# Score products in three reduced-precision passes from the second unit on, and a smaller fixed cost for VectorE in the planner

## The chip, the core and the metric

The kernel runs on one core of a Trainium2 chip. The metric is the device time of one execution in microseconds (us). A core has a matrix engine (TensorE, PE in the profile, with its weight loads as PEld), VectorE (DVE), ScalarE (ACT), GpSimd (POOL) and a queue engine (SyncE, SP) that issues the transfers between main memory and the on-chip buffers. Every engine works through its own list of instructions in order and waits on semaphores where it needs the result of another.

## The reference

Causal attention for 4 batches and 12 heads over 448 positions with head size 64, and behind it a feed-forward layer with a hard-swish gate. All is float32.

```python
scores = scale * np.matmul(q, k.transpose(0, 1, 3, 2))
scores = np.where(mask, -1000000000.0, scores)
scores = scores - np.max(scores, axis=-1, keepdims=True)
attn = np.exp(scores)
attn = attn / (np.sum(attn, axis=-1, keepdims=True) + 1e-09)
attn_out = np.matmul(attn, v)
...
x = attn_out.transpose(0, 2, 1, 3).reshape(B * S, H * D)   # 1792 x 768
h = x @ w_in                                                # 768 x 2048
g = h * np.clip(h + 3.0, 0.0, 6.0) / 6.0
out = g @ w_out                                             # 2048 x 768
```

## The kernel before

**Groups and units.** The 1792 rows are cut into tiles of 112. Four groups of 448 rows (the columns of the matrix products) go through the feed-forward layer one after another; group 0 holds the first tile of each batch. Its attention (`first_pair`, six pairs of heads) makes the head of the program. The attention of the later groups is cut into units (`unit(g, p)`, six for each of groups 1 to 3, one for each pair of heads), and the program lays these between the matrix products of the groups before, so that TensorE has work all the time.

**A unit.** Loads of q and k into a buffer `qk` and of v into `vr`; score products in four blocks (two tiles of the unit at a time, two heads; lines 507 onwards) into PSUM banks (all PSUM tiles have the name `b`); a mask with a row minimum on VectorE (L555); exponentials on ScalarE (L562); row sums inverted on VectorE; probabilities scaled by them on GpSimd or VectorE (L582); transposed on TensorE (L594), copied out of PSUM, and multiplied by v on TensorE (L529). In a *raw* unit (`at < N_RAW`) the scores are plain float32 products of `qk`. In the other units ScalarE or GpSimd first rounds `qk` to a high half and VectorE or GpSimd subtracts that for a low half (both in the type fp32r), and the scores are three products: high by high, high by low, low by high.

**Feed-forward weights.** They come in *chunks*, 16 of `w_in` and 24 of `w_out` for each group; a chunk is counted here from 0 in group 0. In group 0 a chunk lands in two buffers `wd`, VectorE puts its bits in order in three steps of two instructions (L642, L644, L647, with a PSUM bank for what lies between), ScalarE casts it to `wh` (L284), GpSimd or VectorE subtracts for `wl` (L296), and TensorE multiplies (L668, L669, L670: three matmuls make a *triple*; a chunk of `w_in` takes six triples, 18 matmuls). After each chunk of `w_in` ScalarE makes a relu (L691) and VectorE the gate (L697), which gives the product's PSUM bank free; two products have a bank at a time.

**What sets the order.** Every operation has a due key, the engines that may take it (with a cost factor and a delay after which an engine may help), a planned duration, and the buffers that it needs. `Flow.run` plays the program through before it is built: an engine takes the due operation with the smallest key whose inputs and buffers are there. That gives each engine its list, which the chip then follows in order. Planned durations of VectorE come from `elem`, those of the mask have 0.2 us more. `unit` gets its keys from `T_EARLY` and the other constants. The plan is nothing but an order: what runs on the chip waits by semaphores, for the instructions themselves.

**Queues.** All loads and stores go out on SP in one order; SP's issue of a transfer waits until the transfer eight places before it has landed. Names: `d` is a common set of on-chip buffers, `gh` and `gl` hold the halves of the gated result (and, at first, q and k and v of group 0), `kept_w` is a copy of the ordered weights in main memory for the later groups, `r` a buffer for results taken out of PSUM, `prow` the row statistics.

Of the kernel before, what the change touches and what calls it, by code (L numbers as in the profile page):

```python
# [16 lines left out]
B, H, S, D = 4, 12, 448, 64  # L17
DM, DFF = 768, 2048
C = 112
# [8 lines left out]

T_FIRST, T_EARLY, T_EACH, T_LATE, T_DENSE, T_LOAD, T_W, T_WLOAD = -66, 8, 13, 84, 7, -24, 9, 9
T_XA, T_X, T_LAST, T_PAIR, T_SUMS = 156, 178, 192, 10.5, 190
T_SECOND, T_PRODUCT = T_LAST + 8 * T_PAIR, 12

N_RAW = 7
T_V, T_W0 = 9,23
NORM_LAG = 1

BUFS = dict(
    gh=1, gl=1, prow=4, r=4, kl=3, vr=3, wh=3, wl=3, pr2=3, pr1=3, wd=6, d=22,  # L40
# [5 lines left out]
    qk="d qk", op="d op", wf="d wf", x="d x", pt="d pt", pr3="d pr3", xq="d xq", xc="d xc", gt="d gt", so="d so",  # L46
    ps="b s most ps", tp="b s most", av="b s", mo="b mo", c="b c",
)
MOST = dict(qk=4, op=4, wf=4, x=8, pt=5, pr3=2, xq=6, xc=21, gt=12, so=3, s=6, most=6, ps=6, mo=2, c=8)

ORDERED = dict(wd=0, wh=1, wl=2, xq=3, xc=3, gt=3, pr3=4, pr2=5, pr1=6, pt=7, op=8)

# [176 lines left out]
def tile_causal_attention_hardswish_moe(ctx: ExitStack, tc: tile.TileContext, q, k, v, w_in, w_out, out):  # L229
    nc = tc.nc  # L230
# [14 lines left out]

    flow = Flow({**BUFS, **BANKS, **MOST})

    def buf(tag, shape, dt=F32):
        return Buf(tag, shape, dt)

    def bank(tag):
        return Buf(tag, [128, 512], F32)

    def ap(b):
        if b.tile is None:
            b.tile = pools[b.tag].tile(b.shape, b.dt, tag=b.tag, name=b.tag)
        return b.tile
# [5 lines left out]
    def one(key, ways, dur, emit, r, w, port=True):  # L263

        ways = {e: x if isinstance(x, tuple) else (x, 0) for e, x in ways.items()}
        o = flow.op(key, ways, [(dur, emit, w)], r)
        if not port:
            o.port = set()

    def pe(key, parts, r, tiled=False):  # L270
        flow.op(key, {"PE": (1, 0)}, [(d, lambda e, g=g: g(), w) for d, g, w in parts], r, tiled)
# [3 lines left out]
        flow.op(key, {queue: (1, 0)}, [(0.1, lambda e: start(out=o(), in_=i()), w)], r, nbytes=nbytes)  # L275

    def elem(n, psum=False):
        return (n + 150) / 960

    def move(key, n, o, i, r, w, ways=None, scale=None):  # L280

        def emit(e):
            if e == "A":
                nc.scalar.copy(o(), i()) if scale is None else nc.scalar.mul(o(), i(), scale)  # L284
            elif e == "D":
                if scale is None:
                    nc.vector.tensor_copy(o(), i())
                else:
                    nc.vector.tensor_scalar(o(), i(), scale, None, ALU.mult)
            else:  # L290
                nc.gpsimd.tensor_scalar(o(), i(), 1.0, 1.0, ALU.mult, ALU.mult)
        one(key, ways or {"A": 1}, (n + 200) / 1200, emit, r, w)

    def minus(key, n, o, a, b, r, w, ways, op=ALU.subtract):
        def emit(e):
            (nc.gpsimd if e == "P" else nc.vector).tensor_tensor(o(), a(), b(), op)  # L296
        one(key, ways, elem(n), emit, r, w)
# [43 lines left out]
    def first_pair(p):  # L341
# [36 lines left out]
        for e in (1, 0):  # L378
            one(
                t + 1, {"D": 1}, elem(S), lambda _, e=e: nc.vector.tensor_reduce(row(e, 0), sc[e](), AX.X, ALU.max),  # L380
                [(ps[e], 0)], [(st, e, 0)],
            )
            if e:
                one(
                    t + 1, {"D": 1}, .25,
                    lambda _: nc.vector.tensor_scalar(row(1, 0), row(1, 0), -0.125, None, ALU.mult),
                    [], [(st, 1, 0)], False,
                )
        for b in range(B):
# [8 lines left out]
        allb = [(pr, 0, b) for b in range(B)]  # L398
        one(
            t + 2, {"D": 1}, elem(S), lambda _: nc.vector.tensor_tensor(pb[0](), sc[0](), wide(0, 0), ALU.subtract),  # L400
            [(ps[0], 0), (st, 0, 0)], allb,
        )
# [56 lines left out]
    def row_of(pr, e, i):  # L459
        x = ap(pr[e, i])  # L460
        return x[:, e] if i == NC_ - 1 else x

    def unit(g, p):
        at = NPAIR * (g - 1) + p
        raw32 = at < N_RAW
        t = T_EARLY + T_EACH * at if g == 1 else T_LATE + T_DENSE * (at - NPAIR)
        av, off = bank("av"), 0
        stages, turns, pieces, deps = [], [], [], []
        for u, (b, tiles, groups) in enumerate(UNITS[g]):
# [3 lines left out]
            qk = buf("qk", [128, R + S])  # L473
            for src, c0, c1, n in ((q, C * lo, 0, nq), (k, 0, nq, nk)):
                for h in range(2):
# [3 lines left out]
                        w=[(qk, h, bool(c1))],  # L479
# [4 lines left out]
            if not raw32:  # L484
                hi_lo, key = [buf("op", [128, R + S], F32R) for _ in range(2)], t - 5 + 2 * u
# [6 lines left out]
            st = buf("prow", [C, 2, 8])  # L492
            ps = {(e, i): bank("ps") for i in tiles for e in range(2)}
# [19 lines left out]
            pt = {}  # L513
            pairs = [buf("pt", [C, 2, S]) for _ in groups]
            for e in range(2):
                for js, ph in zip(groups, pairs):
                    blocks = [(i, j) for j in js for i in range(max(j, lo), hi)]
                    o = 0
                    for j in js:
                        w = C * (hi - max(j, lo))  # L520
# [18 lines left out]
        for a in range(0, len(stages), 2):  # L539
            two, key = stages[a:a + 2], t + a  # L540
            cost, more = (1.68e-3, .17) if raw32 else (1.362e-3, .05)
            for few in [two]:
                pe(
                    key,
                    [(cost * C * (i + 1) + more, lambda i=i, go=go: go(i), [(ps[0, i], 0), (ps[1, i], 0), ("turn",)])
                     for _, i, go, ps, *_ in few],
                    [x for z in few for x in z[6]] + [("unit", at - 2)], True,
                )
            for u, i, _, ps, pr, st, *_ in two:
                w = C * (i + 1)  # L550
                for e in range(2):
                    dst = lambda e=e, i=i, w=w, ps=ps: ap(ps[e, i])[:C, :w]
                    one(
                        key + .1, {"D": 1}, elem(w) + .2,
                        lambda _, e=e, i=i, w=w, dst=dst, st=st: nc.vector.tensor_tensor_reduce(  # L555
                            dst(), dst(), mask[:, S - w:], -0.125, 3.0e38, ALU.add, ALU.min, ap(st)[:, e, i:i + 1]
                        ),
                        [], [(ps[e, i], 0), (st, e, i)],
                    )
                    one(  # L560
                        key + .2, {"A": 1}, (w + 300) / 1200 + .25,
                        lambda _, e=e, i=i, dst=dst, st=st, pr=pr: nc.scalar.activation(  # L562
                            row_of(pr, e, i), dst(), ACTF.Exp, bias=ap(st)[:, e, i:i + 1], scale=-1.0,
                            accum_out=ap(st)[:, e, 4 + i:5 + i],
                        ),
                        [(ps[e, i], 0), (st, e, i)], [(pr[e, i], e), (st, e, 4 + i)],
                    )

        for u, (b, tiles, _) in enumerate(UNITS[g]):
            st, pr = [(z[5], z[4]) for z in stages if z[0] == u][0]  # L570

            def inverse(_, st=st, tiles=tiles):
                r = ap(st)[:, :, 4 + tiles[-1]:5 + tiles[0]]
                nc.vector.tensor_scalar_add(r, r, 1e-9)
                nc.vector.reciprocal(r, r)  # L575

            one(t + 4, {"D": 1}, .45, inverse, [], [(st, e, 4 + i) for e in range(2) for i in tiles], False)
            for e in range(2):
                for i in reversed(tiles):
                    def scaled(w, e=e, i=i, st=st, pr=pr):  # L580
                        x = row_of(pr, e, i)
                        (nc.gpsimd if w == "P" else nc.vector).tensor_scalar(  # L582
                            x, x, ap(st)[:, e, 4 + i:5 + i], 1.0, ALU.mult, ALU.mult
                        )
                    one(
                        t + 4.5 + .1 * e + .2 * u, {"P": 1, "D": (.6, NORM_LAG)}, .2 + C * (i + 1) / 1000, scaled,
                        [(st, e, 4 + i)], [(pr[e, i], e)],
                    )
        for c, (e, u, blocks, pr, ph, w, st) in enumerate(turns):
            tp, key = bank("tp"), t + 6 + .9 * c  # L590

            def turn(e=e, blocks=blocks, tp=tp, pr=pr):
                for o, (i, j) in enumerate(blocks):
                    nc.tensor.transpose(ap(tp)[:C, C * o:C * o + C], row_of(pr, e, i)[:, C * j:C * j + C], ident)  # L594

            pe(key, [(.1 * len(blocks), turn, [(tp, 0)])], [(pr[e, i], e) for i in sorted({i for i, _ in blocks})])
            move(
                key + .1, w, lambda ph=ph, e=e, w=w: ap(ph)[:, e, :w], lambda tp=tp, w=w: ap(tp)[:C, :w],
                [(tp, 0)], [(ph, e)], {"A": 1} if raw32 else {"A": 1, "D": (1, .4)},
            )  # L600
        pe(t + 15.9, pieces, deps, True)
        if g < 2:
# [436 lines left out]
    for g in range(2):  # L1039
        if g:  # L1040
            for p in range(NPAIR):
                unit(g, p)
        group(g)
    for g in (2, 3):
        for p in range(NPAIR):
            unit(g, p)
# [7 lines left out]
    with tc.manual_schedule():  # L1054
        for _, _, e, emit, port in order:
            traced = nc.cur_bb.bb.instructions
            n = len(traced)
# [42 lines left out]
```

## Time and profile before

| what | value |
|---|---|
| median of 3 runs | 613.27 us (612.43 to 614.84) |
| the profiled execution's own time | 614.25 us |
| its span in the trace | 612.5 us |
| mean granted TensorE clock | 0.989 |
| TensorE busy | 599.6 us, 98% of the span |
| VectorE busy | 470.2 us, 77% |
| ScalarE busy | 365.9 us, 60% |
| GpSimd busy | 269.1 us, 44% |

The span is what the trace covers; the run's own time has 1.75 us more around it. [...]

### The profile page before, as it was taken

To read this page: it belongs to the slowest core of one execution; us is meant where nothing else is said; L and a number is where in the kernel's file an instruction comes from. 1 tells how busy PE (TensorE), PEld (TensorE's weight loads), DVE (VectorE), ACT (ScalarE), POOL (GpSimd) and SP (SyncE) were. 2 spreads that over 40 slices of the span, in tenths; PEclk is the share of its full clock that TensorE was granted. 3 is DMA by queue.
4 is the path that set the end of the run, shared out by engine and by line. 5 is a ranking of instruction groups with operands and counts; after the bars stand their busy time and mean duration, and the time that the engine had idled before them with its cause. 6 is when DMAs were issued, how large, how long until landed. Compare 5 with 4: busy or idle time off the path is not lost.

```text
span 612.5 us, 11307 instructions
## 1 busy us (share of the span) xinstructions
PE 599.6 (98%) x3724; PEld 522.2 (85%) x3724; DVE 470.2 (77%) x1044; ACT 365.9 (60%) x846; POOL 269.1 (44%) x277
## 2 busy tenths in 40 slices
PE   7799999999999999999999999999999999999997
PEld 5577888887888888888888888899999999999996
DVE  5879987887796876688786755588778878898861
ACT  3955757655555767776576655375545575446630
POOL 1767785654676347655184161005554343010000
PEclk8979999999999999999999999999999999999999
DMA  9969986988898654444365344435554367583321
GB/s 207 258 176 331 336 270 229 331 254 287 262 289 255 196 172 143 138 137 142 109 173 166 118 127 133 126 117 176 166 167 162 121 196 241 164 261 114 116 68 54
DMA packets 79738, 114.68 MB, mean 187 GB/s; under 512 B 20736, under 2 KB 55488, under 8 KB 79680
## 3 DMA queue, kind: packets, MB, share of 16 engines
q1 hardware_dynamic: 79248, 113.80, 61.2%
q8 instruction: 29, 0.48, 0.3%
q14 instruction: 29, 0.24, 0.1%
q10 hardware_dynamic: 432, 0.17, 0.1%
HBM read 86.80 MB, written 27.13 MB: 186 GB/s over the span
## 4 chain that ended last, share of the span: by engine, by line
PE 92%; DMA 2%; DVE 2%; ACT 2%; POOL 1%; SPq 1%; issue 0%; DVEq 0%; POOLq 0%
PE b L668 24%; PE b L669 23%; PE b L670 23%; PE b L594 7%; PE b L507 7%; PE b L529 7%; DMA gh<-in_k_dram 1%; SPq L275 1%; DMA wd<-in_w_in_dram 1%; PE b L430 1%; ACT d L284 0%; PE b L373 0%; ACT d L392 0%; POOL d L582 0%; POOL d L421 0%
## 5 line engine op out<-in xcount | busy, mean ns | idle before, releaser
L668 PE MATMUL b<-d,wh 128*128 128x448 f32 x504 | 187.4, 372 | 1.0 <-DVE r L697 1.0
L669 PE MATMUL b<-d,wh 128*128 128x448 f32 x504 | 182.9, 363 | 0.0
L670 PE MATMUL b<-d,wl 128*128 128x448 f32 x504 | 182.2, 361 | 0.0
L284 ACT CAST wh<-wd 128x768 fp32r<-128x768 f32 (+1 forms) x92 | 71.5, 778 | 59.1 <-PE b L669 35.2
L668 PEld LDWEIGHTS b<-d,wh 128*128 128x128 f32 x504 | 94.7, 188 | 10.0 <-DVE r L697 1.4
L670 PEld LDWEIGHTS b<-d,wl 128*128 128x128 f32 x504 | 94.4, 187 | 7.0 <-POOL wl L296 0.3
L669 PEld LDWEIGHTS b<-d,wh 128*128 128x128 f32 x504 | 94.8, 188 | 5.0
L555 DVE CUSTOM_DVE_ANT_0 b<-b,mask 112x448 f32<-112x448 f32 (+2 forms) x144 | 69.5, 533 | 29.8 <-PE b L507 29.1
L296 DVE TENSOR_TENSOR wl<-wd,wh 128x768 fp32r<-128x768 f32 (+1 forms) x67 | 59.9, 894 | 32.3 <-ACT wh L284 31.4
L668 PE MATMUL b<-gh,wh 128*128 128x448 f32 x192 | 74.6, 388 | 0.0
L296 POOL TENSOR_TENSOR wl<-d,wh 128x512 fp32r<-128x512 f32 (+1 forms) x38 | 58.5, 1540 | 30.0 <-ACT wh L284 28.7
L670 PE MATMUL b<-gh,wl 128*128 128x448 f32 x192 | 69.7, 363 | 0.0
L669 PE MATMUL b<-gl,wh 128*128 128x448 f32 x192 | 69.7, 363 | 0.0
L296 POOL TENSOR_TENSOR wl<-wd,wh 128x768 fp32r<-128x768 f32 (+1 forms) x25 | 43.5, 1741 | 59.1 <-DVE vr L948 43.5
L284 ACT COPY d<-b 112x336 f32<-112x336 f32 (+2 forms) x110 | 46.5, 454 | 35.5 <-PE b L594 22.1
L562 ACT ACTIVATE pr<-b,prow 112x336 f32<-112x336 f32 (+1 forms) x96 | 47.0, 497 | 9.6 <-DVE prow L555 6.3
L507 PE MATMUL b<-d 64*112 64x448 f32 (+2 forms) x376 | 46.7, 376 | 0.4 <-DVE prow L414 0.4
L582 POOL TENSOR_SCALAR pr<-pr,prow 112x224 f32<-112x224 f32 (+1 forms) x69 | 33.9, 503 | 29.3 <-DVE prow L575 19.7
L529 PE MATMUL b<-d,vr 112*64 112x224 f32 (+2 forms) x504 | 44.9, 329 | 0.0
L529 PEld LDWEIGHTS b<-d,vr 112*64 112x64 f32 x504 | 30.6, 137 | 15.6 <-issue 2.6
L296 POOL TENSOR_TENSOR d<-d 128x560 fp32r<-128x560 f32 (+3 forms) x19 | 28.0, 1473 | 35.9 <-PE b L507 18.3
L594 PE MATMUL b<-ident,pr 112*112 112x112 f32 x240 | 43.2, 262 | 0.0
(110 smaller groups left out, 1072.4 us busy)
## 6 DMA issues: line engine op xcount, KB each, us to landing
wd<-in_w_in_dram SPq DMA_DIRECT2D x32, 384.0 KB, 5.9
wd<-in_w_out_dram SPq DMA_DIRECT2D x24, 512.0 KB, 5.4
wd<-kept_w SPq DMA_DIRECT2D x32, 384.0 KB, 3.5
wd<-kept_w SPq DMA_DIRECT2D x84, 128.0 KB, 3.1
kept_w<-d SPq DMA_DIRECT2D x16, 384.0 KB, 6.5
kept_w<-d SPq DMA_DIRECT2D x24, 256.0 KB, 5.4
wd<-kept_w SPq DMA_DIRECT2D x24, 256.0 KB, 2.8
kept_s<-wd SPq DMA_DIRECT2D x12, 512.0 KB, 3.5
```

What stands on the lines that cost most here:

```text
L275: flow.op(key, {queue: (1, 0)}, [(0.1, lambda e: start(out=o(), in_=i()), w)], r, nbytes=nbytes)
L284: nc.scalar.copy(o(), i()) if scale is None else nc.scalar.mul(o(), i(), scale)
L296: (nc.gpsimd if e == "P" else nc.vector).tensor_tensor(o(), a(), b(), op)
L507: nc.tensor.matmul(ap(ps[e, i])[:C, :w], x[m, c], y[m, nq:nq + w], start=n == 0, stop=n == len(terms) - 1)
L529: nc.tensor.matmul(ap(av)[64 * e:64 * e + 64, off + nq - w:off + nq], ap(vr)[:, j, e, :], ap(ph)[:, e, o:o + w], start=(j == 0), stop=(j = ...
L555: lambda _, e=e, i=i, w=w, dst=dst, st=st: nc.vector.tensor_tensor_reduce(dst(), dst(), mask[:, S - w:], -0.125, 3.0e38, ALU.add, ALU.min, ...
L562: lambda _, e=e, i=i, dst=dst, st=st, pr=pr: nc.scalar.activation(row_of(pr, e, i), dst(), ACTF.Exp, bias=ap(st)[:, e, i:i + 1], scale=-1. ...
L582: (nc.gpsimd if w == "P" else nc.vector).tensor_scalar(x, x, ap(st)[:, e, 4 + i:5 + i], 1.0, ALU.mult, ALU.mult)
L594: nc.tensor.transpose(ap(tp)[:C, C * o:C * o + C], row_of(pr, e, i)[:, C * j:C * j + C], ident)
L668: nc.tensor.matmul(ps, ap(wh)[:, a], xh, start=start, stop=False, skip_group_check=more)
L669: nc.tensor.matmul(ps, ap(wh)[:, a], xl, start=False, stop=False, skip_group_check=more)
L670: nc.tensor.matmul(ps, ap(wl)[:, a], xh, start=False, stop=stop, skip_group_check=more)
```

## The change

The scores of units 1 to 6 become three products of halves, as units 7 to 17 have them already; unit 0 alone stays raw. The planner's fixed part for a VectorE instruction goes from 150 to 130 elements (at 960 elements a microsecond) and the extra of a mask from 0.2 to 0.12 us. Some due keys move by 1 to 4, VectorE may help with scalings after 1.5 instead of 1, and with the copies of a raw unit's transposed tiles too; a ScalarE way for scalings is there with a delay of 99, which it never reaches; one more buffer pair `pt` may be held.

```diff
-T_FIRST, T_EARLY, T_EACH, T_LATE, T_DENSE, T_LOAD, T_W, T_WLOAD = -66, 8, 13, 84, 7, -24, 9, 9
-T_XA, T_X, T_LAST, T_PAIR, T_SUMS = 156, 178, 192, 10.5, 190
+T_FIRST, T_EARLY, T_EACH, T_LATE, T_DENSE, T_LOAD, T_W, T_WLOAD = -66, 5, 13, 80, 7, -24, 9, 8
+T_XA, T_X, T_LAST, T_PAIR, T_SUMS = 154, 177, 192, 10.5, 188
...
-N_RAW = 7
+N_RAW = 1
...
-NORM_LAG = 1
+NORM_LAG, NORM_LAG_A, TP_LAG, TP_LAG_RAW = 1.5, 99, 0.4, 0.4
+
+FIXED, ROWS = 130, 0.12
...
-MOST = dict(qk=4, op=4, wf=4, x=8, pt=5, pr3=2, xq=6, xc=21, gt=12, so=3, s=6, most=6, ps=6, mo=2, c=8)
+MOST = dict(qk=4, op=4, wf=4, x=8, pt=6, pr3=2, xq=6, xc=21, gt=12, so=3, s=6, most=6, ps=6, mo=2, c=8)
...
     def elem(n, psum=False):
-        return (n + 150) / 960
+        return (n + FIXED) / 960
...
-                        key + .1, {"D": 1}, elem(w) + .2,
+                        key + .1, {"D": 1}, elem(w) + ROWS,
...
-                        t + 4.5 + .1 * e + .2 * u, {"P": 1, "D": (.6, NORM_LAG)}, .2 + C * (i + 1) / 1000, scaled,
+                        t + 4.5 + .1 * e + .2 * u, {"P": 1, "D": (.6, NORM_LAG), "A": (1, NORM_LAG_A)}, .2 + C * (i + 1) / 1000, scaled,
...
-                [(tp, 0)], [(ph, e)], {"A": 1} if raw32 else {"A": 1, "D": (1, .4)},
+                [(tp, 0)], [(ph, e)], {"A": 1, "D": (1, TP_LAG_RAW if raw32 else TP_LAG)},
```

The lists of the engines move all over the program, since the plan is played anew. Line numbers in the changed kernel are 2 higher up to the masks (L509 for the score products) and 5 higher behind them (L647, L649, L652 for the bit steps, L673 to L675 for the weight products, L702 for the gate).

On VectorE, at the end of the head, where chunks 3 and 4 are put in order; before:

```order
L642 TENSOR_SCALAR b<-wd 128x384 x2
L644 SCALAR_TENSOR_TENSOR b<-wd,b 128x384 x2
L647 SCALAR_TENSOR_TENSOR d<-wd,b 128x384 x2
L697 SCALAR_TENSOR_TENSOR r<-r,b 128x448
L642 TENSOR_SCALAR b<-wd 128x384 x2
L644 SCALAR_TENSOR_TENSOR b<-wd,b 128x384 x2
L647 SCALAR_TENSOR_TENSOR d<-wd,b 128x384 x2
L697 SCALAR_TENSOR_TENSOR r<-r,b 128x448
L555 ISA b,prow<-b,mask 112x224
```

The same place on VectorE in the changed kernel, first the steps of chunk 3, then those of chunk 4:

```order
L289 CAST d<-b 128x448
L647 TENSOR_SCALAR b<-wd 128x384 x2
L649 SCALAR_TENSOR_TENSOR b<-wd,b 128x384 x2
L652 SCALAR_TENSOR_TENSOR d<-wd,b 128x384 x2
L647 TENSOR_SCALAR b<-wd 128x384 x2
L649 SCALAR_TENSOR_TENSOR b<-wd,b 128x384 x2
L652 SCALAR_TENSOR_TENSOR d<-wd,b 128x384 x2
L702 SCALAR_TENSOR_TENSOR r<-r,b 128x448 x2
L557 ISA b,prow<-b,mask 112x224
```

The gates of chunks 0 and 1 stood behind chunk 3 and behind chunk 4; now both stand behind chunk 4, and a cast of attention results stands ahead.

On TensorE, at the four last score products of unit 0 and the first triple of chunk 2 behind them; before (in brackets the engines and transfer queues whose semaphores the instruction waits for):

```order
L507 MATMUL b<-d 112x224 [waits Activation_49]
L507 MATMUL b<-d 112x224 [waits DVE_49]
L507 MATMUL b<-d 112x224 [waits DMAHW7_49,DMAHW5_49,Activation_49]
L507 MATMUL b<-d 112x224 [waits DMAHW6_49,DMAHW0_49,Activation_49]
L668 MATMUL b<-d,wh 128x448 [waits DVE_49]
L669 MATMUL b<-d,wh 128x448
L670 MATMUL b<-d,wl 128x448 [waits Pool_49]
```

The same place on TensorE in the changed kernel:

```order
L509 MATMUL b<-d 112x224 [waits Activation_49] x2
L509 MATMUL b<-d 112x224 [waits DMAHW7_49,DMAHW5_49,DVE_49]
L509 MATMUL b<-d 112x224 [waits DMAHW0_49,DMAHW6_49,DVE_49,PE_49]
L673 MATMUL b<-d,wh 128x448 [waits DVE_49,PE_49]
L674 MATMUL b<-d,wh 128x448
L675 MATMUL b<-d,wl 128x448
```

The counts behind these semaphores say for which instruction: before, L668 waits for the first gate (L697); now the third and the fourth score product wait for the two last bit steps of chunk 3 (L652), and L673 for the first L652 of chunk 4, whose PSUM bank it takes over. Ahead of this place TensorE has the same 36 matmuls of chunks 0 and 1; before, 12 triples stood behind all work of the head, and now 2 triples each stand ahead of and behind the first score products of unit 0, and 8 behind the head.

On TensorE, one of the blocks of scores of unit 1 (tiles of 448 and 336 columns), before and then in the changed kernel, from the two lists:

```order
L507 MATMUL b<-d 112x448 [waits DMAHW4_49,DMAHW2_49,Activation_49]
L507 MATMUL b<-d 112x448 [waits DMAHW5_49,DMAHW3_49,Activation_49]
L507 MATMUL b<-d 112x336 [waits DVE_49] x2
```

```order
L509 MATMUL b<-d 112x448 x6
L509 MATMUL b<-d 112x336 [waits Activation_49] x2
L509 MATMUL b<-d 112x336 x4
```

Four float32 products became twelve products of halves, and the transfers that the first waited for are now waited for by the engine that makes the halves.

## Rows read from the trace of the kernel before

**Rows 1.** The page, its first part: busy time, share of the span, instructions.

```profile
PE 599.6 (98%) x3724; PEld 522.2 (85%) x3724; DVE 470.2 (77%) x1044; ACT 365.9 (60%) x846; POOL 269.1 (44%) x277
```

**Rows 2.** Busy time by stage: stretch, its length, each engine, granted clock, DMA share, GB/s.

```profile
0.00:38.56 38.56, 30.58 (x260) 23.03 (x260) 29.04 (x70) 22.87 (x77) 18.28 (x24) 0.82 0.90 209
38.56:47.98 9.42, 8.43 (x47) 7.31 (x45) 5.97 (x13) 6.11 (x16) 5.63 (x4) 1.00 0.84 274
47.98:388.91 340.93, 340.72 (x2322) 286.12 (x2322) 264.05 (x680) 219.59 (x558) 189.11 (x203) 1.00 0.66 207
```

**Rows 3.** Timeline of TensorE: start, duration, instruction, [idle before and its releaser].

```profile
45.97 1.01 PE L507 MATMUL b<-d 64*112 64x224 f32 x8
47.98 0.48 PE L668 MATMUL b<-d,wh 128*128 128x448 f32 x1 [0.99 <-DVE r L697]
```

**Rows 4.** Timeline of TensorE around two blocks of float32 scores.

```profile
55.38 1.57 PE L507 MATMUL b<-d 64*112 64x448 f32 x8
56.89 0.47 PE L668 MATMUL b<-d,wh 128*128 128x448 f32 x1
57.20 0.36 PE L669 MATMUL b<-d,wh 128*128 128x448 f32 x1
...
73.75 1.01 PE L507 MATMUL b<-d 64*112 64x224 f32 x8
74.70 0.50 PE L529 MATMUL b<-d,vr 112*64 112x336 f32 x2
```

**Rows 5.** Timeline of TensorE around two blocks of three-product scores.

```profile
244.78 1.31 PE L507 MATMUL b<-d 64*112 64x448 f32 x12
246.02 0.31 PE L594 MATMUL b<-ident,pr 112*112 112x112 f32 x1
...
246.39 0.45 PE L668 MATMUL b<-d,wh 128*128 128x448 f32 x1
246.68 0.37 PE L669 MATMUL b<-d,wh 128*128 128x448 f32 x1
...
268.73 1.02 PE L507 MATMUL b<-d 64*112 64x336 f32 x12
269.68 0.50 PE L594 MATMUL b<-ident,pr 112*112 112x112 f32 x3
```

**Rows 6.** Timeline of VectorE where chunk 3 is put in order.

```profile
43.35 0.56 DVE L642 TENSOR_SCALAR b<-wd 128x384 int32<-128x384 int32 x1 [1.90 <-DMA wd<-in_w_in_dram]
44.98 0.56 DVE L642 TENSOR_SCALAR b<-wd 128x384 int32<-128x384 int32 x1 [1.06 <-DMA wd<-in_w_in_dram]
45.45 1.02 DVE L644 SCALAR_TENSOR_TENSOR b<-wd,b 128x384 int32<-128x384 int32 x2
46.38 1.01 DVE L647 SCALAR_TENSOR_TENSOR d<-wd,b 128x384 int32<-128x384 int32 x2
47.31 0.61 DVE L697 SCALAR_TENSOR_TENSOR r<-r,b 128x448 f32<-128x448 f32 x1
```

**Rows 7.** Timeline of the SP queue: the two issues of chunk 4.

```profile
41.12 1.16 SPq L275 DMA_DIRECT2D wd<-in_w_in_dram  x2
```

**Rows 8.** The page, part 6: issues, size of one, median us to landing.

```profile
wd<-in_w_in_dram SPq DMA_DIRECT2D x32, 384.0 KB, 5.9
```

**Rows 9.** Timeline of GpSimd: the low halves of the last attention results of group 0.

```profile
40.04 2.28 POOL L296 TENSOR_TENSOR d<-r,d 128x448 fp32r<-128x448 f32 x2
```

**Rows 10.** Busy time in windows of 4 us around the head's end, columns as in Rows 2.

```profile
28.00:32.00 4.00, 2.14 (x21) 1.38 (x17) 2.73 (x8) 3.45 (x11) 2.98 (x4) 0.78 0.58 142
32.00:36.00 4.00, 4.00 (x13) 2.71 (x14) 4.00 (x10) 0.00 (x0) 3.56 (x3) 0.50 0.44 105
36.00:40.00 4.00, 4.00 (x44) 3.48 (x43) 2.76 (x10) 3.65 (x8) 1.78 (x1) 0.87 0.51 144
...
44.00:48.00 4.00, 3.01 (x20) 2.23 (x18) 3.02 (x7) 1.79 (x3) 0.85 (x1) 1.00 1.02 404
```

**Rows 11.** Busy time in the first 12 us after the head, columns as in Rows 2.

```profile
49.00:61.00 12.00, 12.00 (x62) 10.20 (x60) 11.97 (x31) 6.91 (x18) 10.62 (x10) 1.00 0.87 310
```

More of the change, by code (lines that the diff above doesn't have):

```diff
@@ L581, in scaled @@
                         x = row_of(pr, e, i)
+                        if w == "A":
+                            nc.scalar.mul(x, x, ap(st)[:, e, 4 + i:5 + i])
+                            return
                         (nc.gpsimd if w == "P" else nc.vector).tensor_scalar(
```

## The prediction

> **What bounds the kernel now.** I read the page's busy times first. TensorE is busy for 98% of the span, VectorE for 77%, the others less [rows 1]. That is an average, so I cut the span into stages next, by the place where TensorE last waits. In the head, to 38.56 us, TensorE is busy for 30.58 us; in the next 9.42 us for 8.43; and from 47.98 to 388.91 us for 340.72 of 340.93 [rows 2]. So from 48 us on, everything on TensorE's list is paid for in full, an instruction saved there is time saved, and work of other engines costs nothing as long as it doesn't make TensorE wait. Ahead of 48 us it is the other way round: TensorE waits for others, and its list is short of work. The last of these waits is the one to look at. At 45.97 TensorE begins the four last score products of unit 0, and at 47.98 chunk 2 begins, 0.99 us late, released by VectorE's gate [rows 3]. Whatever moves the start of chunk 2 moves all that comes after it.
>
> **The scores on TensorE.** A block of float32 scores with tiles of 448 and 336 columns goes from 55.38 to the next instruction at 56.89, 1.51 us; one with 224 and 224 from 73.75 to 74.70, 0.95 us [rows 4]. Three products take 1.24 us for 448 and 336 columns (244.78 to 246.02) and 0.95 us for 336 and 224 (268.73 to 269.68) [rows 5]. For 224 and 224 no row exists. From 784 to 560 columns the time falls by 0.29 us, 1.3 ns a column, so 448 columns should take 0.95 - 112 x 0.0013 = 0.80 us. A unit of the first group of units then saves 0.27 + 0.15 = 0.42 us. Unit 6 has blocks of another cut, and I give it the same. Six units save 2.5 us. The bound below is what the first block alone saves, 6 x 0.27 = 1.6 us; the bound above has the small block save as much as the big one, 6 x 0.54 = 3.2 us.
>
> The order of TensorE's work changes too: the weight matmuls stand in 105 runs instead of 107, and the transpositions in 77 instead of 89. The first matmul of a run takes longer to the next one's start: 0.31 us behind scores (56.89 to 57.20) and 0.29 us behind transpositions (246.39 to 246.68) [rows 4, 5], so it hardly matters which work stands ahead. I put that at plus 0.1 us, and the whole at **-2.4 us**.
>
> [...]
>
> **VectorE ahead of chunk 2.** This is the place that I think decides. In the trace the two halves of chunk 3 land just ahead of 43.35 and 44.98, since VectorE's first steps on them begin there after waits for the transfer, and the six steps run until the gate of chunk 0 begins at 47.31 [rows 6]. In the changed list that gate stands behind the six steps of chunk 4 as well. Nor does chunk 4 come sooner: its two loads are issued from 41.12 on [rows 7], the order of the SP queue is the same up to there, and a load of these takes 5.9 us to land [rows 8], so the halves come at about 47.0 and 47.6, when VectorE is just through with chunk 3. Steps follow each other at 0.93 us for two, 0.465 us each (45.45, 46.38, 47.31 [rows 6]).
>
> What chunk 2's first matmul needs is, by the semaphore's count, the first L652 of chunk 4, whose PSUM bank it takes. That is the fifth step: it begins at 47.31 + 4 x 0.465 = 49.17 and ends 0.56 us later, at 49.73 (the 0.56 us is the duration of a single step [rows 6]). With a semaphore's passing chunk 2 begins at 49.8 instead of 47.98: **+1.8 us**. At most it waits for the gate of chunk 0 (47.31 + 6 x 0.465 + 0.61 = 50.7: +2.7 us); at least the banks are had in time, which is a rival below.
>
> Is TensorE there in time? Ahead of this place it has the same 36 matmuls and the same score products. The low halves of the last attention results are written by GpSimd until 42.3 (40.04 + 2.28 [rows 9]); behind them stand at most 12 triple parts of the two chunks, 12 matmuls at 0.2 us (57.20, and so on at the pace of [rows 4]), so TensorE could be through with the 36 by about 44.7. In the trace they end at 45.97, when the scores begin [rows 3]. So TensorE is not late, it is up to 1.3 us early, and waits the longer. The four score products don't shorten that: by their counts the third and the fourth wait for the last steps of chunk 3, which begin at 46.38.
>
> **The clock.** From 44.7 to 49.8 TensorE then has only the 0.95 us of scores, some 4 us of waiting. In the head the granted clock fell from 1.00 to 0.78, 0.50 and 0.87 in three windows of 4 us. This came in and behind a window in which TensorE was busy for 2.14 of 4 us; in the window 44 to 48, with 3.01 us busy, it stayed at 1.00 [rows 10]. The changed kernel's windows there come to about 1.7 us busy, nearer to the first. The fall in the trace is worth (0.22 + 0.50 + 0.13) x 4 = 3.4 us of full-speed work, if TensorE has work all through it; part of it lies in the waits that caused it. I take **+3.0 us**, with bounds 0 (the clock stays) and 3.4.
>
> **The other engines.** Units 1 to 6 need 12 casts on ScalarE and GpSimd and 12 subtractions (9 on GpSimd, 3 on VectorE), of which no row prices the effect on TensorE. They're hidden as long as the ordered weights are ready before TensorE wants them. That cover is thin right behind the head: from 49 to 61 us VectorE is busy for 11.97 of 12 us and GpSimd for 10.62 [rows 11]. By the two lists VectorE gets ten more items there before the steps of chunk 9: two casts, a copy, a subtraction and six scalings. But TensorE comes there 2 to 5 us late itself, which gives them as much. I take 0; without that cover they cost what they last, at most 10 x 0.6 = 6 us with the gate's duration [rows 6] for each. The planner's smaller fixed part has no time of its own on the chip; it acts through these orders alone.
>
> **The sum**, against the profiled execution's own 614.25 us: -2.4 + 1.8 + 3.0 = +2.4, so 616.65 us. The median of the runs shown is 1.0 us below that execution, so I forecast a median of **615.7 us**.
>
> **The rivals.**
> - *The wait without the clock.* If the head's work is spread so that the clock stays at 1.00, only the wait and the saved scores are left: -2.4 + 1.8 = -0.6, a median of 612.7 us. For it speaks that the 0.99 us wait of [rows 3] left the clock alone; against it, that the wait is several times as long.
> - *Chunk 2 doesn't wait* (faster). This needs chunk 4 in place some 2 us sooner, so that the steps of both chunks are over by 46 us. Then TensorE goes from the scores right into chunk 2 at 45.7 instead of 47.98, and the total changes by -2.3 - 2.4 = -4.7: 608.6 us. It decides from the moment that the second half of chunk 4 lands before about 44 us. Against it stand the issue at 41.12 and the 5.9 us [rows 7, 8].
> - *VectorE becomes the bound behind the head.* Nothing of the +1.8 and +3.0 us is lent to it, as it is what delays TensorE; its ten items push the weights of chunks 5 to 9 back, by about 3.5 us in all if an item takes a little over half of the 0.61 us of a gate [rows 6]; from there on TensorE waits, once the late start has no room left. The sum would be 616.65 + 3.5, a median of 619.2 us. For it speaks the full VectorE of [rows 11]; against it, that the later chunks of group 0 stand behind attention work which TensorE has to do anyway.
>
> [...]
>
> **How the numbers follow.** The forecast (wait and clock) 0.50, the wait without the clock 0.25, no wait 0.13, VectorE as the bound 0.12. The forecast's own bounds are 614 (less of the clock) to 617.5 us (the wait for the gate, and all of the clock). The range goes from the lower part of the no-wait case, of which I leave out about half, to that of VectorE's: 609.5 to 619 us. What a measurement here can tell from no change is about 0.5%, 3.1 us, so faster is below 610.2 and slower above 616.3. Faster: the no-wait case and a little of the second, 0.15. Slower: about half of the forecast's half and nearly all of VectorE's case, 0.36. The same: 0.49.
>
> **What the changed kernel's profile would show.** Chunk 2's first weight matmul at about 49.8 us after a wait for VectorE; the gates of chunks 0 and 1 behind it; a granted clock of 0.5 to 0.9 in a window between 48 and 60 us; blocks of scores with 448 and 336 columns at 1.24 us where they took 1.51, with 224 and 224 at about 0.80; hardly any wait of TensorE behind that. I am wrong if chunk 2 begins before 48 us, if the clock stays at 1.00, or if TensorE waits for `wl` or `wh` more than once or twice between 50 and 100 us.

## The result and the profile after

The changed kernel takes 622.41 us (median of 6 runs, 619.17 to 625.36) where the kernel before takes 613.08 us (6 runs): slower by 1.5%, a ratio of 1.015 with a 95% interval of 1.013 to 1.017. I had forecast 615.7 us, in a range that ended at 619.

The profiled execution took 619.17 us, with a span of 617.4 us. First the page's busy times, and the first line of its part 4, the shares of the engines in the chain of work that ended last.

```profile
PE 595.2 (96%) x3772; PEld 521.6 (84%) x3772; DVE 495.2 (80%) x1068; ACT 357.5 (58%) x825; POOL 285.9 (46%) x298
...
PE 84%; DVE 8%; DMA 5%; ACT 1%; issue 1%; SPq 0%; POOL 0%; DVEq 0%; ACTq 0%
```

TensorE is busy for 4.4 us less than in [rows 1], and the span is 4.9 us longer: it waits more, and VectorE and transfers have 13% of the chain. The same stages as in [rows 2] say where (length, then PE, PEld, DVE, ACT, POOL, granted clock):

```profile
0.00:38.56 38.56, 26.74 (x266) 20.18 (x268) 30.82 (x71) 23.24 (x76) 19.75 (x24) 1.00 0.92 213
38.56:47.98 9.42, 7.52 (x42) 5.33 (x38) 6.47 (x17) 5.38 (x14) 4.87 (x4) 1.00 0.92 308
47.98:388.91 340.93, 336.11 (x2340) 286.20 (x2342) 277.59 (x691) 210.82 (x539) 209.06 (x225) 0.99 0.67 203
```

In the long stage, where TensorE was busy all the time before, 4.8 us are now missing. The timeline of TensorE shows the two places where it waits longest in that stage, chunk 2 and a chunk of `w_out`, and below them two blocks of three-product scores of the units that were raw, each with what follows it:

```profile
48.75 0.44 PE L673 MATMUL b<-d,wh 128*128 128x448 f32 x1 [1.87 <-DVE d L652]
...
121.09 0.48 PE L673 MATMUL b<-gh,wh 128*128 128x448 f32 x1 [3.63 <-ACT d L286]
...
75.78 0.88 PE L509 MATMUL b<-d 64*112 64x224 f32 x12
76.59 0.47 PE L673 MATMUL b<-d,wh 128*128 128x448 f32 x1
...
110.53 1.32 PE L509 MATMUL b<-d 64*112 64x448 f32 x12
111.79 0.47 PE L673 MATMUL b<-d,wh 128*128 128x448 f32 x1
```

The scores are as cheap as forecast: 0.81 us for 224 and 224 columns (75.78 to 76.59) and 1.26 us for 448 and 336 (110.53 to 111.79), against 0.95 and 1.51 us in [rows 4]. Chunk 2 waits for a bit step, as forecast. The wait of 3.63 us at 117.5 us is new, and nothing in my prediction stands for it. TensorE waits for ScalarE there, and ScalarE's timeline says for what:

```profile
106.18 0.83 ACT L286 CAST wh<-d 128x768 fp32r<-128x768 f32 x1 [1.67 <-DVE d L652]
...
115.42 0.43 ACT L286 COPY d<-b 112x336 f32<-112x336 f32 x1
120.60 1.12 ACT L286 COPY d<-b 112x336 f32<-112x336 f32 x3 [4.74 <-DMA kept_w<-d]
```

The copy takes transposed probabilities out of PSUM, and PSUM banks stay taken until it is done. It waits for a store to `kept_w`: by the semaphore's count for that of chunk 15, whose ordered weights were in the buffer `d` that the copy is to write. The SP queue's timeline around it:

```profile
110.68 1.10 SPq L277 DMA_DIRECT2D d<-in_q_dram  x2
111.83 1.23 SPq L277 DMA_DIRECT2D d<-in_k_dram  x2
113.16 1.01 SPq L277 DMA_DIRECT2D wd<-in_w_out_dram  x2
114.22 0.42 SPq L277 DMA_DIRECT2D kept_w<-d  x1
```

ScalarE's cast of chunk 15 begins at 106.18 us, so the ordered weights were there; the store was issued at 114.22, behind four loads of q and k and two of weights, and the copy that waited for it began at 120.60. Behind this wait the clock falls (windows of 4 us, columns as in [rows 2]):

```profile
116.00:120.00 4.00, 1.45 (x12) 1.14 (x11) 2.12 (x4) 0.00 (x0) 2.84 (x4) 1.00 0.95 321
120.00:124.00 4.00, 2.91 (x19) 2.29 (x19) 1.62 (x5) 3.40 (x9) 1.16 (x1) 0.79 1.03 414
124.00:128.00 4.00, 4.00 (x20) 3.59 (x19) 3.12 (x9) 1.57 (x8) 2.53 (x4) 0.78 0.60 228
```

That is (0.21 + 0.22) x 4 = 1.7 us. The granted clock is a share of full speed: over 122.4 to 125.7 us it is 0.50, and weight matmuls of 448 columns start 0.37 us apart there (124.87 to 125.24), where they start 0.20 us apart at 1.00 (76.90 to 77.10). So this execution's 4.9 us are: chunk 2 later by 0.77, this wait 3.63, the clock 1.72, the scores -2.4, and 1.2 us in small pieces. A theory has to account for more, 9.3 us of medians. The difference comes from the two executions that were profiled: this one is the fastest of six, 3.2 us below its median, and that of the kernel before is 1.2 us above its own, with a granted clock of 0.989 that only 1 of 68 later executions of that kernel shares. So sums against its rows can come out smaller than differences of medians, in all that follows.

### The profile page after: what moved, and what is told of

It reads as the page before. It is cut to its first block, busy times and chain, and to the rows that moved or that the text cites. A ratio compares the mean times of both kernels' runs of the same rounds, so it can differ in the third digit from the quotient of the medians.

```text
span 617.4 us, 11453 instructions
## 1 busy us (share of the span) xinstructions
PE 595.2 (96%) x3772; PEld 521.6 (84%) x3772; DVE 495.2 (80%) x1068; ACT 357.5 (58%) x825; POOL 285.9 (46%) x298
## 4 chain that ended last, share of the span: by engine, by line
PE 84%; DVE 8%; DMA 5%; ACT 1%; issue 1%; SPq 0%; POOL 0%; DVEq 0%; ACTq 0%
PE b L673 22%; PE b L675 21%; PE b L674 21%; PE b L531 7%; PE b L599 6%; PE b L509 6%; DMA kept_w<-d 2%; DVE b L647 2%; DVE b L649 1%; DMA wd<-in_w_out_dram 1%; DVE d L652 1%; DMA wd<-in_w_in_dram 1%; DVE prow L382 1%; DVE b L557 1%; DMA d<-in_k_dram 1%
## 5 line engine op out<-in xcount | busy, mean ns | idle before, releaser
L673 PE MATMUL b<-d,wh 128*128 128x448 f32 x504 | 186.5, 370 | 1.9 <-DVE d L652 1.9
L675 PE MATMUL b<-d,wl 128*128 128x448 f32 x504 | 183.1, 363 | 0.0
L673 PEld LDWEIGHTS b<-d,wh 128*128 128x128 f32 x504 | 94.5, 187 | 11.0 <-issue 3.4
L675 PEld LDWEIGHTS b<-d,wl 128*128 128x128 f32 x504 | 94.6, 188 | 5.5
L298 DVE TENSOR_TENSOR wl<-wd,wh 128x768 fp32r<-128x768 f32 (+1 forms) x75 | 69.1, 923 | 27.3 <-ACT wh L286 25.9
L673 PE MATMUL b<-gh,wh 128*128 128x448 f32 x192 | 75.1, 391 | 3.6 <-ACT d L286 3.6
L298 POOL TENSOR_TENSOR wl<-d,wh 128x512 fp32r<-128x512 f32 (+1 forms) x40 | 60.9, 1523 | 28.2 <-ACT wh L286 26.9
L675 PE MATMUL b<-gh,wl 128*128 128x448 f32 x192 | 70.2, 366 | 0.0
L286 ACT COPY d<-b 112x336 f32<-112x336 f32 (+3 forms) x92 | 38.6, 448 | 39.8 <-PE b L599 25.2
L298 POOL TENSOR_TENSOR wl<-wd,wh 128x768 fp32r<-128x768 f32 (+1 forms) x17 | 28.7, 1686 | 67.3 <-PE b L675 32.8
L298 POOL TENSOR_TENSOR d<-d 128x560 fp32r<-128x560 f32 (+4 forms) x28 | 42.2, 1508 | 27.5 <-ACT d L286 13.4
L564 ACT ACTIVATE pr<-b,prow 112x224 f32<-112x224 f32 (+1 forms) x96 | 46.8, 494 | 12.7 <-DVE prow L557 7.3
L286 ACT CAST wh<-d 128x512 fp32r<-128x512 f32 (+1 forms) x40 | 28.4, 710 | 32.5 <-DVE d L652 32.5
L587 POOL TENSOR_SCALAR pr<-pr,prow 112x336 f32<-112x336 f32 (+1 forms) x73 | 37.1, 519 | 21.3 <-DVE prow L577 15.2
L509 PE MATMUL b<-d 64*112 64x224 f32 (+2 forms) x424 | 44.0, 337 | 0.6 <-DVE d L652 0.6
L673 PEld LDWEIGHTS b<-gh,wh 128*128 128x128 f32 x192 | 36.3, 189 | 9.5 <-ACT d L286 3.9
```

Source lines behind the costliest of these rows:

```text
L509: nc.tensor.matmul(ap(ps[e, i])[:C, :w], x[m, c], y[m, nq:nq + w], start=n == 0, stop=n == len(terms) - 1)
L587: (nc.gpsimd if w == "P" else nc.vector).tensor_scalar(x, x, ap(st)[:, e, 4 + i:5 + i], 1.0, ALU.mult, ALU.mult)
L673: nc.tensor.matmul(ps, ap(wh)[:, a], xh, start=start, stop=False, skip_group_check=more)
L675: nc.tensor.matmul(ps, ap(wl)[:, a], xh, start=False, stop=stop, skip_group_check=more)
```

## The experiments

Two theories. **Store**: TensorE loses most where a copy waits for a buffer that a late store holds; more halves in the common buffers (the set `d`) bring this about. **Cost**: the smaller planned costs of VectorE put the lists in an order that runs late on the chip, whatever the scores. Beside them stood the step of my prediction, here the **head** theory: the gate behind chunk 4 and the clock. All kernels below were timed against the kernel before on the same chip.

**The costs alone**, on the kernel before.

```diff
-        return (n + 150) / 960
+        return (n + 130) / 960
...
-                        key + .1, {"D": 1}, elem(w) + .2,
+                        key + .1, {"D": 1}, elem(w) + .12,
```

> The kernel before with nothing but the smaller planned VectorE costs (fixed part 130, mask extra 0.12); seven raw units stay. Store theory (TensorE lost 3.6 us at 117.5 us because a copy out of PSUM waited for a buffer that the late store of chunk 15 still held, and 1.7 us to the clock behind it; six more units with halves make these buffers scarce): about as before, 611 to 615 us, and no wait of several us behind 50 us. Cost theory (the smaller planned costs put VectorE's list in an order that runs late on the chip): most of the loss is here, 618 to 623 us.

616.65 us against 613.25, ratio 1.0066 (1.0046 to 1.0087). Neither theory has it: a third of the loss is here. TensorE's start of chunk 2, and the windows of 4 us behind it:

```profile
49.55 0.44 PE L668 MATMUL b<-d,wh 128*128 128x448 f32 x1 [2.55 <-DVE d L647]
```

```profile
48.00:52.00 4.00, 2.45 (x8) 2.22 (x9) 4.00 (x12) 2.33 (x6) 2.25 (x2) 0.77 1.03 416
52.00:56.00 4.00, 4.00 (x17) 3.66 (x17) 3.01 (x9) 1.49 (x6) 2.93 (x3) 0.80 0.86 279
```

This is the mechanism of the head theory: the smaller costs put both gates behind chunk 4, chunk 2 begins 1.57 us later than in [rows 3], and the clock costs (0.23 + 0.20) x 4 = 1.7 us. The sum is 3.3 us. The medians differ by 3.4 us, the two profiled executions by 2.3, so the sum is right to about 1 us.

**The scores alone**, on the kernel before (the scaling lag is needed for the plan to find an order).

```diff
-N_RAW = 7
+N_RAW = 1
...
-NORM_LAG = 1
+NORM_LAG = 1.5
```

> The kernel before with three products in units 1 to 6 and, since the plan finds no order otherwise, the help of VectorE with scalings after 1.5 instead of 1; old costs. Store theory: six more units hold halves in the common buffers, so a wait for a store of ordered weights shows up on TensorE here too: 615 to 622 us. Cost theory: only the saved score time is left, 610 to 612 us.

615.07 us, ratio 1.0034 (1.0016 to 1.0051). Slower without the new costs, at the lower end of the store theory's range; but the wait is another one, and no wait for a store holds TensorE up. TensorE's timeline and the clock behind it:

```profile
98.55 0.38 PE L594 MATMUL b<-ident,pr 112*112 112x112 f32 x2 [0.50 <-DVE d L647]
100.86 0.38 PE L594 MATMUL b<-ident,pr 112*112 112x112 f32 x2 [1.93 <-DVE d L647]
```

```profile
100.00:104.00 4.00, 3.05 (x12) 2.67 (x13) 3.70 (x13) 2.96 (x10) 3.91 (x4) 0.80 0.95 294
104.00:108.00 4.00, 4.00 (x20) 2.91 (x20) 0.99 (x3) 0.68 (x2) 2.64 (x4) 0.77 1.04 352
```

Transpositions wait for PSUM banks in which VectorE has weights half ordered; VectorE itself waited for a store for only 0.33 us there. The 2.4 us of wait and 1.7 us of clock eat the 2.4 us of the scores and more. So the scores' own order costs too, by a wait for VectorE.

**The store taken away.** The changed kernel in its own order; the store of chunk 15 reads a constant tile of zeros, so the later groups get nothing from chunk 15.

```diff
...
-            dma(t - T_W, 512 * n, lambda: kept[i, :, :n], w, wk, [("kept", i)])
+            if i == 15:
+                dma(
+                    t - T_W, 512 * n, lambda: kept[i].rearrange("p (a b) -> p a b", b=128),
+                    lambda: zero.unsqueeze(1).to_broadcast([128, 6, 128]),
+                    wk, [("kept", i)],
+                )
+            else:
+                dma(t - T_W, 512 * n, lambda: kept[i, :, :n], w, wk, [("kept", i)])
```

> The changed kernel in its own order, but the copy of chunk 15 that is kept for the later groups is stored from a constant tile of zeros, so that no buffer is held for it (groups 1 to 3 then get nothing from chunk 15; the work is the same). Store theory: the wait of 3.6 us at 117.5 us goes, the clock stays at 1.00 there, and the median falls by about 5 us to 616 to 618 us. Cost theory: no change, 620 to 624 us; the wait comes back within a few us, for another releaser.

615.25 us, ratio 1.0033 (1.0016 to 1.0049): 7 us less than the changed kernel, and a little more gained than I had expected. No wait of TensorE over 0.4 us is left behind chunk 2.

**The planner told of the landing time.**

```diff
-    DMA_RATE, DMA_LATENCY = 260e3, 2.5
+    DMA_RATE, DMA_LATENCY = 260e3, 6.0
```

> The changed kernel with the planner told that a transfer lands 6.0 us behind its place in the queue instead of 2.5 us (the store of chunk 15 took 6.3 us in the trace). Store theory: the planner no longer takes buffers for free that a store still holds, the long wait behind 50 us goes: 612 to 618 us. Cost theory: VectorE's list is as late as before: 620 to 625 us.

639.12 us, ratio 1.0416 (1.0381 to 1.0451). Missed by both theories; the plan that comes out is much worse. Waits of TensorE behind 45 us, by what is waited for (total, times, longest):

```profile
PE b L673 <- DVE vr L298: 5.3, 5, 2.0
PE b L673 <- ACT d L286: 2.8, 1, 2.8
PE b L675 <- DVE wl L298: 2.6, 4, 1.2
```

ScalarE's copies still hold TensorE up once, for 2.8 us. Most of the rest is that VectorE's instructions on results (`vr`) and the low halves of the weights (`wl`) now come late, five times for 5.3 us and four times for 2.6. A truer number in one place of the planner wasn't a better plan here.

**The store moved, nothing left out.** In the order as planned, the four loads of q and k go behind the store of chunk 15 in the SP queue (`at` finds the operations of a name in that order).

```diff
...
+    behind = at(("store", 15))[0]
+    loads = [n for n in range(behind) if order[n][2] == "SP"][-6:-2]
+    order[behind + 1:behind + 1] = [order[n] for n in loads]
+    for n in reversed(loads):
+        del order[n]
```

> The changed kernel with nothing but the place of one transfer changed: the store of chunk 15 (with the two loads of weights that stand ahead of it) goes ahead of the four loads of q and k that it stood behind in the SP queue; no work is left out. Store theory (the copy out of PSUM at 120.6 us waited for this store): the store is issued at about 110.7 instead of 114.2 us and lands by 117, the wait of TensorE of 3.6 us and the clock's fall behind it go, 615 to 617 us. Cost theory (VectorE's list runs late): 620 to 624 us.

615.33 us, ratio 1.0038 (1.0023 to 1.0054); the changed kernel on the same chip took 622.57. The SP queue and ScalarE now:

```profile
110.54 0.33 SPq L278 DMA_DIRECT2D kept_w<-d  x1
```

```profile
116.99 1.51 ACT L289 COPY d<-b 112x336 f32<-112x336 f32 x4 [0.66 <-DMA kept_w<-d]
```

The store goes out 3.7 us sooner, the copies begin at 116.99 instead of 120.60, and the wait of TensorE is gone. Five lines of order are worth 7 us. This settles the store theory for the changed kernel. The late head is still there, as TensorE's start of chunk 2 and the clock behind it show:

```profile
48.46 0.64 PE L676 MATMUL b<-d,wh 128*128 128x448 f32 x1 [1.91 <-DVE d L655]
```

```profile
48.00:52.00 4.00, 3.54 (x10) 3.18 (x11) 4.00 (x12) 3.13 (x8) 2.91 (x3) 0.57 1.03 413
```

**The gate moved** (the bit steps of chunk 4 behind the gate of chunk 0 on VectorE), **both moves**, and **the changed kernel once more**.

```diff
...
+    bits, gate = at(("bits", 4)), at(("gate", 0))[0]
+    moved = [n for n in bits if n < gate]
+    order[gate + 1:gate + 1] = [order[n] for n in moved]
+    for n in reversed(moved):
+        del order[n]
```

> The changed kernel with nothing but one gate moved on VectorE: the gate of chunk 0 goes ahead of the six bit steps of chunk 4, where it stood in the kernel before. Head theory (the first step of the prediction): chunk 2 begins by 47 us instead of 48.75, the clock has no reason to fall there, and the median falls by 2 to 4 us, to 618 to 620.5 us; the wait at 117 us stays. If the head costs nothing: 621 to 624 us.

> The changed kernel with both moves, the store of chunk 15 and the gate of chunk 0. If the two stalls are the whole loss, what is left is the saved score time: 610.5 to 613 us, under the kernel before. If a third loss exists, 614 us or more.

> The changed kernel once more, for a second profile and for runs on the same chip as the three others: 619 to 625 us, with the wait of about 3.6 us for the store of chunk 15 in the profile. The head theory expects a fall of the clock in some windows before 56 us in most executions.

The gate alone: 620.68 us, ratio 1.0122 (1.0100 to 1.0145), 1.9 us less than the changed kernel, which the two intervals don't tell from nothing; and chunk 2 began at 48.30 us, not by 47, with 1.7 us of clock lost behind it. Both: 616.75, ratio 1.0057 (1.0037 to 1.0077), not better than the store alone: a miss. By my own expectation that means a third loss. The changed kernel again: 622.57, ratio 1.0139 (1.0105 to 1.0172). Its second profile, of an execution of 621.03 us, shows the head nearly as forecast, in TensorE's timeline and the windows of 4 us:

```profile
50.03 0.71 PE L673 MATMUL b<-d,wh 128*128 128x448 f32 x1 [2.60 <-DVE d L652]
```

```profile
48.00:52.00 4.00, 1.97 (x5) 1.84 (x6) 4.00 (x12) 2.27 (x5) 2.22 (x2) 0.61 1.03 413
52.00:56.00 4.00, 4.00 (x13) 3.57 (x12) 3.25 (x10) 1.80 (x6) 4.00 (x4) 0.53 0.71 255
```

Chunk 2 begins at 50.03 us (I had said 49.8), and the clock's fall is worth (0.39 + 0.47) x 4 = 3.4 us; at a clock of 0.50, the lowest in [rows 10], a mean of 0.61 over 48 to 52 us has the fall begin at 48.9 us. That is an estimate; by it the fall begins 1.1 us ahead of chunk 2, so 0.5 us of this lies in the wait, and 2.9 us are left (I had said 3.0). In the kernel with both moves chunk 2 still began at 47.73, since the gate's input, ScalarE's relu, stood behind a cast that waits for chunk 3:

```profile
45.65 0.83 ACT L289 CAST wh<-d 128x768 fp32r<-128x768 f32 x1 [2.98 <-DVE d L655]
46.39 1.15 ACT L705 ACTIVATE r<-b,three 128x448 f32<-128x448 f32 x2
```

Behind the head that kernel has one long wait of TensorE, and its clock stays at 1.00 through both of its waits of 2 us:

```profile
60.81 0.31 PE L602 MATMUL b<-ident,pr 112*112 112x112 f32 x1 [2.00 <-POOL pr L590]
```

So I moved **the relu** too, and beside it tried what brings the store's wait: **five buffer pairs** `pt` instead of six, and **seven raw units** with all else as changed.

```diff
...
+    relu = at(("relu", 0))[0]
+    cast = [n for n in range(relu) if order[n][2] == "A"][-1]
+    order.insert(relu, order.pop(cast))
```

> The kernel with both moves and, on ScalarE, the relu of chunk 0 ahead of the cast of chunk 3, behind which it waited until 46.4 us in the profile of the kernel with both moves. Head theory: the relu runs at about 44, the gate at 45.6, chunk 2 begins by 46.8 us (47.73 before this move), VectorE has chunk 4 in order as early as in the changed kernel, so that the wait of 2.0 us at 60.8 us for GpSimd's scaling goes too; the median falls to 611 to 613.5 us. If the order of the head is not what costs: 615.5 to 618 us.

> The changed kernel with five buffer pairs for transposed tiles, as before, instead of six; the plan is played anew. If the sixth one brings the copies into buffers that a store still holds, the long wait behind 50 us goes, 614 to 617 us. If the halves of six more units make the buffers scarce, it stays, 619 to 625 us.

> The changed kernel with seven raw units, so the scores as before and all constants as changed. If the halves of six more units bring the wait for a store: it is gone here, the head's loss is left as in the run with the costs alone, and the saved score time is not there: 615 to 618 us. If the constants bring it: 620 to 626 us.

With the relu moved: 616.21 us, ratio 1.0061 (1.0047 to 1.0074). Missed, though chunk 2 begins at 46.03, with no wait at all. Part of what was gained comes back 12 us later, as TensorE's timeline, the clock and GpSimd's timeline show:

```profile
58.48 0.31 PE L602 MATMUL b<-ident,pr 112*112 112x112 f32 x1 [1.37 <-POOL pr L590]
```

```profile
60.00:64.00 4.00, 4.00 (x19) 3.56 (x18) 3.96 (x11) 2.36 (x9) 3.23 (x3) 0.57 0.96 301
```

```profile
53.19 1.90 POOL L301 TENSOR_TENSOR d<-d 128x784 fp32r<-128x784 f32 x1
55.03 1.87 POOL L301 TENSOR_TENSOR wl<-d,wh 128x768 fp32r<-128x768 f32 x1
56.85 1.15 POOL L301 TENSOR_TENSOR gl<-r,gh 128x448 fp32r<-128x448 f32 x1
57.96 0.47 POOL L590 TENSOR_SCALAR pr<-pr,prow 112x224 f32<-112x224 f32 x1
```

The subtraction for the low halves of a unit that was raw (`d<-d`), 1.9 us on GpSimd, stands ahead of the scaling that the transpositions wait for, as do those for `wl` and `gl`; that it is this one that makes the scaling late was not tried by itself. TensorE, no longer late, now waits 1.37 us for the scaling, and the clock costs 0.43 x 4 = 1.7 us more. In the changed kernel the same list of GpSimd is covered by the late head: there the scaling begins at 58.92, and TensorE comes for it only at 59.64.

This is not the whole third loss. Against the rows of before, chunk 2 is 1.95 us sooner, the scores save 2.4, TensorE waits 1.9 us more behind chunk 2 and the clock costs 1.7: together -0.75 us, where the span is 1.1 us longer and the median 4.1. For the kernel with both moves the same sum is about 0, where the span is 1.7 us longer and the median 3.8. What is missing I can't place.

Five pairs: 620.61 us, ratio 1.0136 (1.0118 to 1.0154), and the wait is there, as ScalarE's timeline shows:

```profile
120.12 1.12 ACT L286 COPY d<-b 112x336 f32<-112x336 f32 x3 [4.19 <-DMA kept_w<-d]
```

Seven raw units: 615.92 us, ratio 1.0057 (1.0041 to 1.0073), with no wait for the store; chunk 2 begins at 49.31. So with the changed constants it is the halves of the six units that bring the store's wait, not the sixth pair. It takes both: the same halves with the old constants brought no such wait. Which of the constants does it, the costs or the due keys, was not tried.

Last, the **head by itself**: the costs alone, with the gate and the relu moved as above.

> The kernel before with the smaller planned costs alone (616.65 us), and with the relu of chunk 0 ahead of the cast of chunk 3 on ScalarE and its gate ahead of the bit steps of chunk 4 on VectorE; all else in the same order. Head theory (chunk 2's start at 49.55 us and the clock's fall behind it are the whole 3.4 us): chunk 2 begins by 47 us, no fall between 48 and 56 us, and the median falls to 611.5 to 613.5 us. Rival (the time comes back behind the head, as in the kernel with both moves and the relu): 615 to 617 us, with a new wait of TensorE between 50 and 70 us.

613.70 us, ratio 1.0020 (1.0005 to 1.0036): 1.0 us above the kernel before, where the costs alone were 3.4 above, and just outside the 611.5 to 613.5 that I expected. TensorE and the clock:

```profile
46.88 0.48 PE L674 MATMUL b<-d,wh 128*128 128x448 f32 x1 [1.17 <-DVE r L701]
```

```profile
48.00:52.00 4.00, 4.00 (x21) 3.60 (x20) 4.00 (x12) 1.93 (x4) 2.16 (x2) 1.00 1.02 412
52.00:56.00 4.00, 4.00 (x22) 3.75 (x21) 4.00 (x12) 3.21 (x10) 4.00 (x4) 1.00 0.80 229
```

Chunk 2 early, the clock at 1.00, and 2.4 of the 3.4 us back. Here GpSimd has no halves of a raw unit's q and k in its list behind the head, and TensorE's longest wait behind chunk 2 is 0.6 us. No version beat the kernel before.

## Why the prediction was wrong

**What bounds the kernel** was read rightly: what TensorE waits behind 48 us is lost, and the clock's fall, where it follows, with it.

**The scores** (-2.4 us): right. The blocks take 1.26 and 0.81 us; I had 1.24 and 0.80. Against the float32 blocks of 1.51 and 0.95 us that is 0.83 and 0.85.

**VectorE ahead of chunk 2** (+1.8 us) and **the clock** (+3.0 us): the mechanism was right. The smaller planned costs are enough to bring it, as the run with these alone shows, and moving the gate and the relu undoes most of it there. The sizes vary by execution: chunk 2 later by 0.77 and 2.05 us in the two profiles of the changed kernel, the clock behind it 0 and 2.9 us; 1.57 and 1.7 with the costs alone. In the first profile VectorE begins the last four steps of chunk 3 at 44.24 instead of 45.45 us, since the second half landed sooner; in the second it waits twice, 0.26 and 0.39 us, for chunk 4. I had fixed both times from one trace.

**The other engines** ("I take 0"): this step failed. I counted the twelve casts and subtractions as work, looked for engines with room, and priced the missing cover by VectorE's instructions alone. What I left out is that halves take buffers, and that buffers come free by transfers. With the halves, a copy was planned into the buffer of chunk 15, and the store that frees it stood behind loads in SP's list and went out 8 us after its data were there, 3.7 of these for the four loads of q and k. In the place of my 0 the runs show 7.2 us of medians (622.57 to 615.33). The profiles with this wait price it lower: 5.3 us with the clock in the first of the changed kernel, 1.9 in the second and 3.0 with the gate moved, both without a fall of the clock. The second profile's head is later (chunk 2 at 50.03 against 48.75 us), and the chunk that waits for the copies behind the store too (124.19 against 121.09); so head and store don't simply add up. The rest of the 7.2 I can't place.

With that wait away the change costs 615.33 - 612.92 = +2.4 us: the sum of my other steps, +2.4. That they meet is luck. In the profile of that very kernel these steps come to 0.5 for chunk 2, 1.7 for the clock and -2.4 for the scores, -0.2 us in all, against a span that is 0.3 us longer than before. And moving the gate and the relu too did not win the head's share back.

**The rivals.** That VectorE becomes the bound behind the head was the nearest to what happened in its time (619.2 us), and wrong in its cause for the changed kernel: the wait was for a transfer. It comes true in kind, on GpSimd, once the head is mended (both moves, and the run with the relu moved), where I had taken the late head as cover. Its price with the relu moved is 1.4 us and the clock's 1.7.

What in the trace of before could have told me: a load of weights took 5.9 us to land [rows 8], and the planner counts 2.5 us behind the transfer's place in the queue. I used the 5.9 for chunk 4 and did not ask which buffers the planner thereby gives away too early.

## What to carry to other kernels

Where an order is made by a planner, count what an edit holds as well as what it computes: a new buffer in a common set can move others into buffers that a store still reads, and a store's time is its place in the queue plus its landing (here 8 and 6.3 us). A change of a planner's costs, however true, is an edit of every list; read the new lists at the places where the critical engine waits for several things. And when a late start is mended, look further on for the work that it covered, here 12 us later.

## What the runs showed that I had not expected

A wait of TensorE need not be long for the granted clock to fall behind it. With the relu moved, 1.37 us of wait was followed by a clock of 0.57 from 60 to 64 us; with the scores alone, 2.4 us by 0.80 and 0.77 from 100 to 108; in the changed kernel, 3.63 us by 0.79 and 0.78 from 120 to 128. Each of these falls is worth 1.7 us, so the short wait lost more to the clock than by itself. But a wait doesn't bring the fall each time. Two waits of 2.0 us with both moves, 1.9 us for ScalarE's copies in the second profile of the changed kernel, and 3.0 us with the gate moved all left the clock at 1.00. At chunk 2 one and the same list gave 1.00 in one profile and 0.61 and 0.53 in another, after waits of 1.87 and 2.60 us. So the price of a wait can't be read from one profile.

Telling the planner the landing time that the trace shows (6.0 for 2.5 us) made the kernel 26 us slower than before (639.12 against 613.25).
